# Attention, a mixture of eight experts and a cosine feed-forward layer on one core: another opening of attention, earlier reads, gates in other places, weight sums one per turn

## The chip, the cores and the metric

One core of a Trainium2 chip. The metric is the device time in microseconds (us). Before the change three runs gave 1983.06, 1985.64 and 1985.77 us, with a median of 1985.64 us.

## The reference

Three stages follow each other. All of it is float32, but the two matrices of the last stage come as float64.

```python
# attention: 4 batches, 8 heads, 576 positions, 64 wide; window of 128, a slope per head
scores = where(0 <= i - j < 128, q @ k.T / 8 - slope[h] * |i - j|, -1e9)
x = softmax(scores) @ v                     # laid out as 2304 tokens x 512
# mixture: 8 experts, 512 -> 1024 -> 512, weights by 8 rounds of row and column normalisation
P = exp(x @ w_gate - max)
for _ in range(8):
    P /= P.sum(1) + 1e-9;  P /= P.sum(0) + 1e-9;  P *= 2304 / 8
y = sum_e P[:, e] * (relu(x @ w1[e]) @ w2[e])
# feed-forward: 512 -> 2048 -> 512
h = y @ w_in;  out = (h * cos(h)) @ w_out
```

## The kernel before

Everything is written in one function under a manual schedule: each engine runs its instructions in the order in which the code issues them, and a DMA queue starts its transfers in order. Generators (`prep_a`, `prep_b`, `prep_sb`, `convert_f64`, `late_gates`, `sinkhorn` and others) hold side work. Each `yield` in them ends one step, and the main loop takes a step at fixed places, so the number of yields sets how far apart the steps stand in the program.

**Attention** (the loop from L794 on) takes 80 groups of 128 query rows of a pair of heads, two groups to a turn `i` of the loop. A turn issues the scores of its couple (`emit_qk`, TensorE matmuls into PSUM tiles `s`), the exponentials of the couple before (`emit_exp`, ScalarE), the bias and row maximum of its own (`emit_max`, VectorE, which frees the PSUM banks of the scores), `gates`, the product with v of the couple four turns back (`emit_AV`, into `xbank`), transposes of q and k of later head pairs (`heads`, which calls `emit_T`; half of them go to `xbank`, half to the pool `ps_g`), the transposes of the normalised scores three turns back (`emit_PT`, tiles `pt`), the normalisation (`emit_norm`, GpSimd) and `side`. The first scores of turns 1 and 3 use half of `xbank` and a bank of `ps_t`; all others use the two banks of `ps_s`. Heads are loaded two pairs ahead by `load_heads`, which issues two or three DMAs on SyncE's queue.

**Gates** (L367 to L384) are six products of 384 tokens with `w_gate`. `gate_block` multiplies and copies to SBUF (`lT`), `gate_block2` transposes and copies to `logits`. `gates(n)` finishes the block of the turn before and starts the next in the same turn. What attention leaves over (two blocks) is done by `late_gates` (L1248), and `sinkhorn` (L386) makes the eight rounds: a row step of four VectorE instructions (L407 to L410), a column sum on TensorE (L417), a column step of four VectorE instructions (L418 to L423).

**Mixture, first token block** (768 tokens; 32 units of 256 hidden columns). The first product uses seven sub-products instead of eight (`product`, in the order 5, 1, 4 of the unit before, 2, 3, 6, a batch, 7); every fp32 product is three matmuls of a high and a low part. A batch (`batch`, `g2`) is 36 matmuls of the second product of the unit before, for six row tiles, each followed by an accumulation on VectorE (`evac`, L1175 or L1185). Beside this the weights of later units are prepared and stored: `prep_s` sums and `prep_a` splits the first matrix into `waX` (the unit's own products read it right after the batch), `prep_b` splits the second into `wbX` (high part on ScalarE, L159, low part on GpSimd, L161), and `prep_sb` makes four sums on GpSimd (L181, "weight sums" below), their high part on ScalarE (L184), their low part on VectorE (L186), the store and the next load. The stored parts serve the later token blocks.

`convert_f64` turns float64 words into float32 with four VectorE instructions and one on ScalarE; its chunks are loaded by `load_f64` as raw 64-bit words.

Of the kernel before, what the change touches and what calls it, by code (L numbers as in the profile page):

```python
# [9 lines left out]
F32 = mybir.dt.float32  # L10
F32R = mybir.dt.float32r
I32 = mybir.dt.int32
U32 = mybir.dt.uint32
# [5 lines left out]
P = 128  # L19
# [10 lines left out]
def tile_attention_moe_cos_ffn(ctx, tc, q, k, v, w_gate, w1, w2, w_in, w_out, out):  # L30
# [41 lines left out]
    with tc.manual_schedule():  # L72
# [82 lines left out]
        def prep_b(u):  # L155
            rb = raw_t[u, "b"]
            wb = wb_of(u)
            yield
            nc.scalar.activation(out=wb[:, :, 0], in_=rb, func=AF.Copy)  # L159
            yield  # L160
            nc.gpsimd.tensor_tensor(out=wb[:, :, 1], in0=rb, in1=wb[:, :, 0].bitcast(F32), op=ALU.subtract)  # L161
            yield
            yield
            d = pair_rows(u)
            for m, f, o in ((1, 0, 0), (2, 1, 0), (4, 1, FU)):
                nc.sync.dma_start(out=d[:, SO.index(m)], in_=wb[:, f, :, o:o + FU].bitcast(F32))
            yield
# [3 lines left out]
        def prep_sb(u):  # L171
# [7 lines left out]
            for o, x, y, op in ((0, a21, a22, ALU.add), (2, raw[:, 0], a11, ALU.subtract),  # L179
                                (3, a11, a21, ALU.subtract), (1, a12, raw[:, 2], ALU.subtract)):  # L180
                nc.gpsimd.tensor_tensor(out=raw[:, o], in0=x, in1=y, op=op)  # L181
                if o in (2, 1) or not u:
                    yield
            nc.scalar.activation(out=hl[:, :, 0], in_=raw, func=AF.Copy)  # L184
            yield
# [6 lines left out]
            yield  # L192
# [61 lines left out]
        def convert_f64(c):  # L254
# [8 lines left out]
            yield  # L263
            nc.scalar.activation(out=a, in_=a, func=AF.Relu, scale=2.0 ** 23, bias=ebias)
            yield
# [4 lines left out]
            yield  # L270
            nc.vector.tensor_scalar(
                out=b, in0=hi, scalar1=0xFFFFF, scalar2=0x100000, op0=ALU.bitwise_and, op1=ALU.bitwise_or
            )
            yield
            nc.vector.scalar_tensor_tensor(
                out=w, in0=lo.bitcast(U32), scalar=2.0 ** -32, in1=b, op0=ALU.mult, op1=ALU.add
            )
# [5 lines left out]
            load_f64(c + 1)  # L283
# [238 lines left out]
        def emit_qk(n, pi, u):  # L522
            a = n % 2
            if n // 2 not in sbank:
                if n // 2 in (1, 3):
                    sbank[n // 2] = [xbank[:, :512], ps_t.tile([P, 512], F32, tag="t", name=f"s{n}_1")]
                else:
                    sbank[n // 2] = [ps_s.tile([P, 512], F32, tag="s", name=f"s{n}_{j}") for j in range(2)]
# [138 lines left out]
        load_heads(0, v, vt, "v")  # L667
# [57 lines left out]
        load_heads(1, v, vt, "v")  # L725
# [12 lines left out]
        def heads(n, pool=None):  # L738
# [3 lines left out]
            if u < 4 and pi + 1 < NP_ALL:  # L742
                emit_T(pi + 1, u, pool)
                if u == 1:
                    load_heads(pi + 2, q, qraw, "qr")
                if u == 3:
                    load_heads(pi + 2, k, kraw, "kr")

        def side(n):
# [6 lines left out]
            if n == 3:  # L756
                load_f64(0)
# [14 lines left out]
            if 8 <= n < 50 and (chunk or n < 40):  # L772
# [9 lines left out]
        def gates(n):  # L782
            nonlocal gate2, next_half
            for j, lT in gate2:
                gate_block2(j, lT, (ps_g, "g"))
            gate2 = []
            if n < NGR + 6 and next_half < 2 * NB and HB * (next_half + 1) <= done_tok:
# [6 lines left out]
        for i in range(NGR // 2 + 4):  # L794
# [9 lines left out]
            if not i:  # L804
                emit_exp(*pair(0)[0])
                emit_T(0, 1, (ps_t, "t"))
                emit_T(0, 3, (ps_g, "g"))
                emit_max(*pair(0)[1])
            for g in pair(i - 4):
                emit_AV(*g)  # L810
# [15 lines left out]
            for g in pair(i - 3):  # L826
                emit_PT(*g)
# [420 lines left out]
        def late_gates():  # L1248
            bank_ = (LastBank(), "m")
            for j in range(next_half, 2 * NB):  # L1250
                o = (1 + 2 * (j % 2)) * TB
                lT = gate_block(j, bank_, cX[:, o:o + HB])
                yield
                yield
                gate_block2(j, lT, bank_)

# [140 lines left out]
```

## Time and profile before

| what | value |
|---|---|
| three runs | 1983.06, 1985.64, 1985.77 us |
| the profiled execution, its own time | 1983.78 us |
| its span | 1982.0 us |
| PE busy / DVE / ACT / POOL | 99% / 79% / 44% / 49% |
| DMA | 540.05 MB, mean 272 GB/s |

The span runs from the first instruction to the last; 1.78 us of the profiled time lie around it. A busy PE is one whose modelled matmuls touch each other, so the 99% say how little named idle time there is, not how fast the array works. The rows in which the trace names an idle time and what ended it are what this case is read from. Attention takes the first 156 us, the first token block goes on to about 680 us.

### The profile page before, as it was taken

The numbers are of one execution on the slowest core, as the hardware profiler recorded it, in microseconds if no ns is written. First come the engines' busy times: TensorE is split into PE (matmuls) and PEld (weight loads), VectorE is DVE, ScalarE is ACT, GpSimd is POOL, SyncE is SP. The second block draws the span as 40 slices with busy tenths as digits, with TensorE's granted clock in tenths as the row PEclk, the third lists the DMA queues.
The fourth block names the chain that finished last, engine by engine and source line by source line (L and its number), as shares of the span: only waits on it lengthen the run. The fifth ranks groups of instructions, "written<-read, shape, count | busy, mean of one in ns | idle before, by whom it ended". The sixth has DMA issues, their size and how long they took to land.

```text
span 1982.0 us, 31160 instructions
## 1 busy us (share of the span) xinstructions
PE 1958.4 (99%) x10977; PEld 1823.2 (92%) x10977; DVE 1559.7 (79%) x2669; ACT 862.2 (44%) x1617; POOL 967.0 (49%) x939
## 2 busy tenths in 40 slices
PE   8999999999999999999999999999999999999999
PEld 6667899999999999999999999999999999998898
DVE  7885877777777788988988877888877776757766
ACT  6885444444444433333333433333233354554543
POOL 5673566666667545454536622545454523333221
PEclk9999999999999999999999999999999999999999
DMA  7854788888888999999999888999898765565552
GB/s 195 220 141 159 263 311 292 309 303 313 310 289 310 319 340 316 343 338 317 340 327 328 274 281 284 330 341 335 324 308 296 242 222 196 197 218 176 207 192 96
DMA packets 293755, 540.05 MB, mean 272 GB/s; under 512 B 80256, under 2 KB 141792, under 8 KB 286432
## 3 DMA queue, kind: packets, MB, share of 16 engines
q1 hardware_dynamic: 292240, 537.74, 78.6%
q8 instruction: 87, 1.43, 0.3%
q14 instruction: 68, 0.56, 0.1%
q10 hardware_dynamic: 1360, 0.33, 0.1%
HBM read 384.32 MB, written 153.67 MB: 271 GB/s over the span
## 4 chain that ended last, share of the span: by engine, by line
PE 88%; DVE 2%; DMA 1%; issue 0%; SPq 0%; POOL 0%; ACT 0%; ACTq 0%; DVEq 0%; POOLq 0%
PE gT L1105 23%; PE y_moe L966 19%; PE z_moe L966 10%; PE gT L1195 7%; PE gT L1196 7%; PE gT L1194 7%; PE y_ffn L966 5%; PE x_moe L966 5%; PE z_ffn L966 2%; PE x_ffn L966 1%; DMA wbX<-wdp 1%; SPq L96 0%; DVE waX L145 0%; DVE acc_ffn L1175 0%; DVE ta L939 0%
## 5 line engine op out<-in xcount | busy, mean ns | idle before, releaser
L1105 PE MATMUL gT<-hX,wbX 128*128 128x384 f32 x2688 | 538.3, 334 | 0.9 <-DMA wbX<-wdp 0.5
L1105 PEld LDWEIGHTS gT<-hX,wbX 128*128 128x128 f32 x2688 | 471.7, 188 | 3.5 <-DMA wbX<-wdp 1.5
L966 PE MATMUL y_moe<-xtT_moe,waX 128*128 128x384 f32 x1728 | 347.1, 335 | 0.6 <-ACT s_moe L995 0.6
L966 PEld LDWEIGHTS y_moe<-xtT_moe,waX 128*128 128x128 f32 x1728 | 304.3, 188 | 3.7 <-ACT s_moe L995 0.9
L1117 DVE TENSOR_TENSOR acc_moe<-gT,acc_moe 128x384 f32<-128x384 f32 x432 | 237.7, 550 | 77.7 <-PE gT L1105 76.0
L1196 PE MATMUL gT<-wbX,hX 128*128 128x512 f32 x660 | 258.0, 391 | 0.0
L1195 PE MATMUL gT<-wbX,hX 128*128 128x512 f32 x660 | 257.8, 391 | 0.0
L1194 PE MATMUL gT<-wbX,hX 128*128 128x512 f32 x660 | 257.7, 390 | 0.0
L995 ACT ACTIVATE s_moe<-y_moe 128x384 f32<-128x384 f32 x192 | 93.3, 486 | 345.6 <-PE y_moe L966 345.5
L1139 POOL TENSOR_TENSOR hodd<-hodd 128x384 f32<-128x384 f32 x128 | 155.4, 1233 | 139.4 <-DVE hX L1125 70.4
L1139 POOL TENSOR_TENSOR cX<-cX 128x384 f32<-128x384 f32 x128 | 146.6, 1165 | 153.6 <-DVE hX L1125 93.8
L955 POOL TENSOR_TENSOR hX<-cX,hX 128x768 fp32r<-128x768 f32 x44 | 83.5, 1914 | 249.3 <-ACT hX L952 208.6
L132 POOL TENSOR_TENSOR s<-ra 128x256 f32<-128x256 f32 x80 | 62.4, 780 | 251.3 <-DVE waX L145 178.9
L1185 DVE SCALAR_TENSOR_TENSOR acc_moe<-gT,prob,acc_moe 128x512 f32<-128x512 f32 x174 | 129.6, 747 | 37.6 <-PE gT L1196 35.8
L1196 PEld LDWEIGHTS gT<-wbX,hX 128*128 128x128 f32 x660 | 123.8, 188 | 26.0
L1194 PEld LDWEIGHTS gT<-wbX,hX 128*128 128x128 f32 x660 | 123.9, 188 | 25.4 <-DVE acc_ffn L1175 0.6
L1195 PEld LDWEIGHTS gT<-wbX,hX 128*128 128x128 f32 x660 | 123.9, 188 | 24.5
L911 ACT ACTIVATE hX<-cX 128x768 fp32r<-128x768 f32 x64 | 44.0, 687 | 218.7 <-DVE cX L998 218.7
L1125 DVE TENSOR_TENSOR hX<-cX,hX 128x768 fp32r<-128x768 f32 x112 | 132.4, 1182 | 1.1 <-ACT hX L1129 1.1
L1125 DVE TENSOR_TENSOR hX<-hodd,hX 128x768 fp32r<-128x768 f32 x112 | 127.5, 1138 | 0.9 <-ACT hX L1129 0.9
L966 PE MATMUL z_moe<-xtT_moe,waX 128*128 128x384 f32 x576 | 116.4, 335 | 0.4 <-DVE waX L145 0.2
L966 PE MATMUL z_moe<-xtB_moe,waX 128*128 128x384 f32 x576 | 115.9, 335 | 0.0
(210 smaller groups left out, 3771.9 us busy)
## 6 DMA issues: line engine op xcount, KB each, us to landing
waX<-wd SPq DMA_DIRECT2D x264, 512.0 KB, 5.5
wbX<-wdp SPq DMA_DIRECT2D x224, 512.0 KB, 6.5
wd<-waX SPq DMA_DIRECT2D x32, 1792.0 KB, 6.8
wdp<-sb SPq DMA_DIRECT2D x32, 1024.0 KB, 5.8
wdp<-wbX SPq DMA_DIRECT2D x96, 256.0 KB, 4.4
wbX<-wd SPq DMA_DIRECT2D x24, 1024.0 KB, 4.8
waX<-wd SPq DMA_DIRECT2D x88, 256.0 KB, 5.2
ra<-in_moe_w_dram SPq DMA_DIRECT2D x64, 256.0 KB, 7.4
```

Of the source, the lines that this page charges most:

```text
L132: nc.gpsimd.tensor_tensor(out=s4[:, o], in0=x, in1=y, op=op)
L955: eng.tensor_tensor(out=h[:, 1], in0=c, in1=h[:, 0].bitcast(F32), op=ALU.subtract)
L966: nc.tensor.matmul(ps[:, :HB], wa[:, WI[m], wl, kc, :], x[:, xl, kc, :], start=start and kc == 0 and n_ == 0, stop=stop and kc == 1 and n_ ...
L995: nc.scalar.activation(out=t["s", i], in_=ps[:, :HB], func=AF.Copy)
L1105: nc.tensor.matmul(ps[:, :HB], w[:, u, wl, d * P:(d + 1) * P], x[:, xl, u, :], start=m in (1, 5, 2) and n_ == 0, stop=m in (4, 3, 2) and n ...
L1117: nc.vector.tensor_tensor(out=a, in0=ps[:, :HB], in1=a, op=ALU.add)
L1125: nc.vector.tensor_tensor(out=x[:, 1], in0=H[:, q], in1=x[:, 0].bitcast(F32), op=ALU.subtract)
L1139: nc.gpsimd.tensor_tensor(out=H[:, t[0], c], in0=H[:, t[1], c], in1=H[:, t[2], c], op=ALU.subtract)
L1185: nc.vector.scalar_tensor_tensor(out=a, in0=ps, scalar=pe, in1=a, op0=ALU.mult, op1=ALU.add)
L1194: nc.tensor.matmul(ps, hf[f][:, 0, ts], wb[:, f, 0, :], start=f == 0, stop=False)
L1195: nc.tensor.matmul(ps, hf[f][:, 0, ts], wb[:, f, 1, :], start=False, stop=False)
L1196: nc.tensor.matmul(ps, hf[f][:, 1, ts], wb[:, f, 0, :], start=False, stop=f == 1)
```

## The change

- `emit_qk`: turn 1 takes both score banks from `ps_t`, turn 3 both from `ps_s`; `xbank` holds no scores any more.
- Turn 3 issues `emit_PT` ahead of the products with v and of the transposes of q and k; later turns keep it behind them.
- q and k are loaded three pairs ahead; the second pair's v is loaded in turn 2, and the first pair's v, the third pair's q and k and the first raw 64-bit words stand in turn 0.
- `convert_f64`: the second VectorE instruction moves up, the merge of the sign moves down, the next chunk is loaded two steps earlier; the first conversion starts one group later.
- `gates` finishes a block in one turn and starts the next in the following turn.
- `late_gates` has a yield ahead of each block and one behind the first.
- `prep_sb` has one sum per step and a step more ahead of its VectorE instruction, and no yield at its end.
- `prep_b`: the low part is made in two halves of 512 columns.

```diff
@@ prep_b
-            nc.gpsimd.tensor_tensor(out=wb[:, :, 1], in0=rb, in1=wb[:, :, 0].bitcast(F32), op=ALU.subtract)
+            for c in range(2):
+                nc.gpsimd.tensor_tensor(out=wb[:, c, 1], in0=rb[:, c], in1=wb[:, c, 0].bitcast(F32), op=ALU.subtract)
@@ prep_sb
                 nc.gpsimd.tensor_tensor(out=raw[:, o], in0=x, in1=y, op=op)
-                if o in (2, 1) or not u:
-                    yield
+                yield
             nc.scalar.activation(out=hl[:, :, 0], in_=raw, func=AF.Copy)
+            yield
             yield
             nc.vector.tensor_tensor(out=hl[:, :, 1], in0=raw, in1=hl[:, :, 0].bitcast(F32), op=ALU.subtract)
...
                 load_raw(u + 2, "b")
-            yield
@@ convert_f64
+            nc.vector.tensor_scalar(
+                out=b, in0=hi, scalar1=0xFFFFF, scalar2=0x100000, op0=ALU.bitwise_and, op1=ALU.bitwise_or
+            )
+            yield
             nc.scalar.activation(out=a, in_=a, func=AF.Relu, scale=2.0 ** 23, bias=ebias)
+            yield
+            nc.vector.scalar_tensor_tensor(
+                out=w, in0=lo.bitcast(U32), scalar=2.0 ** -32, in1=b, op0=ALU.mult, op1=ALU.add
+            )
             yield
             yield
             nc.vector.scalar_tensor_tensor(
                 out=a, in0=hi, scalar=-2147483648, in1=a, op0=ALU.bitwise_and, op1=ALU.bitwise_or
             )
-            yield
-            nc.vector.tensor_scalar(
-                out=b, in0=hi, scalar1=0xFFFFF, scalar2=0x100000, op0=ALU.bitwise_and, op1=ALU.bitwise_or
-            )
-            yield
-            nc.vector.scalar_tensor_tensor(
-                out=w, in0=lo.bitcast(U32), scalar=2.0 ** -32, in1=b, op0=ALU.mult, op1=ALU.add
-            )
+            load_f64(c + 1)
             yield
...
-            load_f64(c + 1)
@@ emit_qk
-                if n // 2 in (1, 3):
-                    sbank[n // 2] = [xbank[:, :512], ps_t.tile([P, 512], F32, tag="t", name=f"s{n}_1")]
-                else:
-                    sbank[n // 2] = [ps_s.tile([P, 512], F32, tag="s", name=f"s{n}_{j}") for j in range(2)]
+                pool, tag = (ps_t, "t") if n // 2 == 1 else (ps_s, "s")
+                sbank[n // 2] = [pool.tile([P, 512], F32, tag=tag, name=f"s{n}_{j}") for j in range(2)]
@@ ahead of the loop
-        load_heads(0, v, vt, "v")
...
-        load_heads(1, v, vt, "v")
@@ heads
-                    load_heads(pi + 2, q, qraw, "qr")
+                    load_heads(pi + 3, q, qraw, "qr")
...
-                    load_heads(pi + 2, k, kraw, "kr")
+                    load_heads(pi + 3, k, kraw, "kr")
@@ side
-            if n == 3:
-                load_f64(0)
+            if n == 5:
+                load_heads(1, v, vt, "v")
...
-            if 8 <= n < 50 and (chunk or n < 40):
+            if 9 <= n < 50 and (chunk or n < 40):
@@ gates
-            for j, lT in gate2:
-                gate_block2(j, lT, (ps_g, "g"))
-            gate2 = []
-            if n < NGR + 6 and next_half < 2 * NB and HB * (next_half + 1) <= done_tok:
+            if gate2:
+                for j, lT in gate2:
+                    gate_block2(j, lT, (ps_g, "g"))
+                gate2 = []
+            elif n < NGR + 6 and next_half < 2 * NB and HB * (next_half + 1) <= done_tok:
@@ the loop over turns
                 emit_T(0, 3, (ps_g, "g"))
+                load_heads(2, q, qraw, "qr")
+                load_heads(0, v, vt, "v")
+                load_heads(2, k, kraw, "kr")
+                load_f64(0)
                 emit_max(*pair(0)[1])
+            if i == 3:
+                for g in pair(i - 3):
+                    emit_PT(*g)
             for g in pair(i - 4):
                 emit_AV(*g)
...
-            for g in pair(i - 3):
-                emit_PT(*g)
+            if i > 3:
+                for g in pair(i - 3):
+                    emit_PT(*g)
@@ late_gates
                 o = (1 + 2 * (j % 2)) * TB
+                yield
                 lT = gate_block(j, bank_, cX[:, o:o + HB])
                 yield
                 yield
                 gate_block2(j, lT, bank_)
+                if j + 1 < 2 * NB:
+                    yield
```

**TensorE, turn 3 of attention.** `s` and, before, `xbank` on the left are the scores of the turn, `pt` the transposes of normalised scores, `xbank<-ident,qr` and `T<-ident,kr` the transposes of q and k of the third pair, and the last row is the first score of turn 4. Before:

```order
L537 MATMUL s_1_435<-kT_377,qT_189 128x256
L494 MATMUL xbank<-ident,qr_370 128x128 x3
L494 MATMUL T_2_463<-ident,kr_413 128x128 x2
L603 MATMUL pt_468<-ident,sp 128x128 x2
L601 MATMUL pt_468<-ident,sp 128x128
L603 MATMUL pt_471<-ident,sp 128x128
L601 MATMUL pt_468<-ident,sp 128x128
L603 MATMUL pt_471<-ident,sp 128x128
L537 MATMUL s_0_491<-kT_377,qT_189 128x256
```

And with the change:

```order
L535 MATMUL s_1_445<-kT_385,qT_189 128x256
L601 MATMUL pt_463<-ident,sp 128x128 x2
L599 MATMUL pt_463<-ident,sp 128x128
L601 MATMUL pt_466<-ident,sp 128x128
L599 MATMUL pt_463<-ident,sp 128x128
L601 MATMUL pt_466<-ident,sp 128x128
L494 MATMUL xbank<-ident,qr_329 128x128 x3
L494 MATMUL T_2_483<-ident,kr_337 128x128 x2
L535 MATMUL s_0_501<-kT_385,qT_189 128x256
```

The transposes into `xbank` move behind the six of `pt`.

**TensorE, start of the first unit of the mixture.** `gT<-xr,wg` is a late gate's product, `gT<-sel,cX` its second step; x, y and z are the unit's sub-products. Before:

```order
L966 MATMUL z_moe_0_2733<-xtT_moe_2000,waX 128x384 x6
L371 MATMUL gT_2732<-xr_87,wg 32x384 x4
L966 MATMUL y_moe_0_2749<-xtB_moe_2051,waX 128x384 x6
L380 MATMUL gT_2732<-sel,cX 128x8 x3
L371 MATMUL gT_2732<-xr_87,wg 32x384 x4
L966 MATMUL x_moe_0_2770<-xtB_moe_2110,waX 128x384 x6
L966 MATMUL z_moe_0_2733<-xtB_moe_2179,waX 128x384 x6
L380 MATMUL gT_2732<-sel,cX 128x8 x3
L966 MATMUL y_moe_0_2749<-xtT_moe_2231,waX 128x384 x6
L966 MATMUL y_moe_0_2749<-xtT_moe_2300,waX 128x384 x6
```

And with the change:

```order
L971 MATMUL z_moe_0_2737<-xtT_moe_2011,waX 128x384 x6
L971 MATMUL y_moe_0_2747<-xtB_moe_2062,waX 128x384 x6
L371 MATMUL gT_2736<-xr_87,wg 32x384 x4
L971 MATMUL x_moe_0_2763<-xtB_moe_2122,waX 128x384 x6
L380 MATMUL gT_2736<-sel,cX 128x8 x3
L971 MATMUL z_moe_0_2737<-xtB_moe_2191,waX 128x384 x6
L971 MATMUL y_moe_0_2747<-xtT_moe_2243,waX 128x384 x6
L371 MATMUL gT_2736<-xr_87,wg 32x384 x4
L971 MATMUL y_moe_0_2747<-xtT_moe_2308,waX 128x384 x6
L971 MATMUL z_moe_1_2808<-xtT_moe_2011,waX 128x384 x6
L380 MATMUL gT_2736<-sel,cX 128x8 x3
```

Each gate step has a sub-product between itself and the one before, and the second product of the gates stands between the last two sub-products.

**VectorE, the batch inside the third unit of the mixture.** `acc<-gT,acc` are the accumulations of the row tiles, L407 to L410 and L418 to L423 the two steps of the normalisation, `waX<-s` the last low part of the next unit's first matrix. Before:

```order
L410 TENSOR_TENSOR prob<-prob,gT_2732 128x144
L1175 TENSOR_TENSOR acc_moe_2889<-gT_2731,acc_moe_2889 128x512
L1175 TENSOR_TENSOR acc_moe_2889<-gT_2729,acc_moe_2889 128x512
L145 TENSOR_TENSOR waX<-ra_1933,waX 128x2x256
L1175 TENSOR_TENSOR acc_moe_2889<-gT_2730,acc_moe_2889 128x512
L145 TENSOR_TENSOR waX<-ra_1933,waX 128x256
L418 TENSOR_REDUCE gT_2732<-gT_2732 128x8
L421 TENSOR_SCALAR gT_2732<-gT_2732 128x8
L422 RECIPROCAL gT_2732<-gT_2732 128x8
L423 SCALAR_TENSOR_TENSOR prob<-prob,gT_2732 128x144
L145 TENSOR_TENSOR waX<-s_3_2932,waX 128x4x256
```

And with the change, from four rows further ahead:

```order
L410 TENSOR_TENSOR prob<-prob,gT_2736 128x144
L1180 TENSOR_TENSOR acc_moe_2888<-gT_2733,acc_moe_2888 128x512
L917 SCALAR_TENSOR_TENSOR hX<-cX,hX 128x768
L1180 TENSOR_TENSOR acc_moe_2888<-gT_2734,acc_moe_2888 128x512
L187 TENSOR_TENSOR sb<-sb 128x4x256
L1180 TENSOR_TENSOR acc_moe_2888<-gT_2735,acc_moe_2888 128x512
L1180 TENSOR_TENSOR acc_moe_2888<-gT_2733,acc_moe_2888 128x512
L418 TENSOR_REDUCE gT_2736<-gT_2736 128x8
L421 TENSOR_SCALAR gT_2736<-gT_2736 128x8
L422 RECIPROCAL gT_2736<-gT_2736 128x8
L423 SCALAR_TENSOR_TENSOR prob<-prob,gT_2736 128x144
L145 TENSOR_TENSOR waX<-ra_1944,waX 128x2x256
```

The low part of the weight sums (`sb`) comes into the batch, behind the second accumulation, in this unit and in all later ones of the block; before it stood between the batches. Behind the rows shown come an accumulation, the second `waX<-ra`, L407 to L410 and then `waX<-s`.

## Rows read from the trace of the kernel before

**Rows 1.** The page's part 1, all engines: busy us (share of the span) x instructions.
```profile
PE 1958.4 (99%) x10977; PEld 1823.2 (92%) x10977; DVE 1559.7 (79%) x2669; ACT 862.2 (44%) x1617; POOL 967.0 (49%) x939
```

**Rows 2.** Windows: engine busy us, then granted TensorE clock, DMA share, GB/s.
```profile
10.00:20.00 10.00, 6.44 (x35) 4.33 (x36) 7.28 (x37) 4.27 (x18) 3.60 (x9) 0.83 0.81 206
...
40.00:60.00 20.00, 20.00 (x172) 13.53 (x171) 16.92 (x77) 19.33 (x61) 12.33 (x24) 1.00 0.67 162
250.00:700.00 450.00, 449.96 (x2281) 409.78 (x2281) 345.28 (x464) 196.12 (x323) 282.54 (x257) 1.00 0.87 307
```

**Rows 3.** Timeline, PE, opening: start, length, work [idle before <-what ended it].
```profile
16.64 0.46 PE L537 MATMUL s<-kT,qT 64*128 64x256 f32 x1
...
18.43 0.55 PE L494 MATMUL xbank<-ident,qr 128*128 128x128 f32 x3 [1.33 <-DVE anb L547]
19.33 0.41 PE L494 MATMUL T<-ident,kr 128*128 128x128 f32 x2 [0.35 <-DMA kr<-in_k_dram]
...
20.33 0.70 PE L537 MATMUL s<-kT,qT 64*128 64x256 f32 x4
...
29.01 0.41 PE L494 MATMUL T<-ident,kr 128*128 128x128 f32 x2 [0.72 <-DMA kr<-in_k_dram]
```

**Rows 4.** Timeline, DVE, opening.
```profile
11.74 0.48 DVE L502 TENSOR_SCALAR qT<-xbank,inv 128x256 f32<-128x256 f32 x1 [0.30 <-PE xbank L494]
...
18.29 0.42 DVE L547 CUSTOM_DVE_ANT_0 sp<-s,rel 128x256 f32<-128x256 f32 x1
```

**Rows 5.** Timeline, PE, middle of attention.
```profile
64.82 0.59 PE L535 MATMUL s<-kT,qL 128*128 128x192 f32 x2 [0.53 <-DVE anb L547]
...
94.76 0.85 PE L371 MATMUL gate<-xr,wg 128*32 128x384 f32 x8 [0.72 <-DVE logits L381]
```

**Rows 6.** Timeline, PE, first unit of the mixture.
```profile
158.20 0.85 PE L371 MATMUL gT<-xr,wg 128*32 128x384 f32 x8 [0.74 <-DVE xr L655]
...
161.21 0.85 PE L371 MATMUL gT<-xr,wg 128*32 128x384 f32 x8 [0.34 <-DVE logits L381]
...
166.73 1.31 PE L966 MATMUL y_moe<-xtT_moe,waX 128*128 128x384 f32 x6 [0.58 <-ACT s_moe L995]
```

**Rows 7.** Timeline, PE, the normalisation's column sums and one product.
```profile
192.42 0.51 PE L417 MATMUL gT<-prob,ones 128*128 128x144 f32 x2 [1.21 <-DVE prob L410]
...
203.05 0.96 PE L966 MATMUL z_moe<-xtT_moe,waX 128*128 128x384 f32 x4 [0.24 <-DVE waX L145]
...
211.33 0.51 PE L417 MATMUL gT<-prob,ones 128*128 128x144 f32 x2 [1.68 <-DVE prob L410]
```

**Rows 8.** Timeline, DVE, same stretch.
```profile
188.56 1.23 DVE L186 TENSOR_TENSOR sb<-sb 128x1024 fp32r<-128x1024 f32 x1 [1.72 <-ACT sb L184]
...
191.19 0.30 DVE L407 TENSOR_REDUCE gT<-prob 128x18 f32<-128x144 f32 x1
...
192.28 0.55 DVE L998 TENSOR_TENSOR cX<-x_moe,s_moe 128x384 f32<-128x384 f32 x1
...
198.46 0.69 DVE L1175 TENSOR_TENSOR acc_moe<-gT,acc_moe 128x512 f32<-128x512 f32 x1 [0.25 <-PE gT L1196]
...
201.78 1.22 DVE L145 TENSOR_TENSOR waX<-s,waX 128x1024 fp32r<-128x1024 f32 x1
```

**Rows 9.** Timeline, a later unit of the first token block: DVE, PE, POOL.
```profile
302.56 1.67 DVE L186 TENSOR_TENSOR sb<-sb 128x1024 fp32r<-128x1024 f32 x1 [0.71 <-ACT sb L184]
...
309.79 0.75 DVE L1185 SCALAR_TENSOR_TENSOR acc_moe<-gT,prob,acc_moe 128x512 f32<-128x512 f32 x1 [0.42 <-PE gT L1196]
...
311.15 0.75 DVE L1185 SCALAR_TENSOR_TENSOR acc_moe<-gT,prob,acc_moe 128x512 f32<-128x512 f32 x1 [0.61 <-PE gT L1196]
...
313.51 1.22 DVE L145 TENSOR_TENSOR waX<-s,waX 128x1024 fp32r<-128x1024 f32 x1
...
314.74 1.20 PE L966 MATMUL z_moe<-xtT_moe,waX 128*128 128x384 f32 x6
314.81 0.74 POOL L132 TENSOR_TENSOR s<-ra 128x256 f32<-128x256 f32 x1 [5.50 <-DVE waX L145]
```

## The prediction

> **What bounds the kernel.** I read the totals first. PE is busy for 99% of the span, DVE for 79%, ACT and POOL for less than half [rows 1]. So a shorter string on another engine is worth nothing by itself: the change, which takes no matmul away, can only give back time in which PE stood still, or take more. Next come the windows [rows 2]. Between 250 and 700 us, where the first token block repeats one unit, PE is busy for 449.96 of 450 us at a granted clock of 1.00. Between 10 and 20 us it is busy for 6.44 of 10 us, at 0.83. Then the timeline, with the idle time ahead of each PE row and what ended it: that is the list of what is to be had, in the opening [rows 3], the middle of attention [rows 5], the first unit of the mixture [rows 6] and the normalisation beside the next units [rows 7]. The VectorE rows beside them [rows 4, 8, 9] say what would be late next.
>
> The sum is made against the profiled execution: 1983.78 us, of which 1982.0 are its span and 1.78 lie around it. The three runs have a median of 1985.64 us; these and the profiled one have a mean of (1983.06 + 1985.64 + 1985.77 + 1983.78) / 4 = 1984.6. One of four runs is as low as the profile, so the same program's typical time is about 0.9 us above the sum's base, and I add that at the end.
>
> **Opening of attention.** Before, turn 3's scores share `xbank` with the transposes of its own turn. The last score ends at 16.64 + 0.46 = 17.10; DVE must then finish the maxes before PE transposes into `xbank` at 18.43, after 1.33 us of idle time; k's transposes wait a further 0.35 for their DMA; the first score of turn 4 starts at 20.33 [rows 3].
> - Turn 2 comes earlier by about the 0.30 us that DVE waited for `xbank` [rows 4]: turn 1's scores no longer hold it. Turn 3's scores then end near 16.8.
> - Between 18.43 and 20.33 PE does `xbank`'s transposes, k's and `pt`: 1.90 us, less the wait for the DMA 1.55. With the change, `pt` comes first and none of it waits for turn 3's maxes, so it ends near 16.8 + 1.55 = 18.35.
> - A new wait stands behind it: turns 3 and 4 now share the two banks of `ps_s`. The last max of turn 3 ends at 18.29 + 0.42 = 18.71 before [rows 4], 18.4 with the earlier turn. So turn 4 starts near 18.45 in place of 20.33: 1.9 us.
> - The 0.72 us at 29.01, a wait for k's DMA [rows 3], goes, since k is loaded three pairs ahead.
>
> Together −2.6. From below, nothing, if these 2.6 us turn into waits for DVE or ACT; from above 2.6 plus (1 − 0.83) x 10 = 1.7 us of half clock [rows 2], if the granted clock returns sooner. I take the clock as it is, because PE still stands still in the first turns. The loads cost no PE time if they land before they are read. q, k and the first raw words are issued in turn 0, the next v's four turns before its product. q's load waits in turn 0 for PE's transposes of the first pair to free its buffer; behind it on SyncE's queue stand v, k and the raw words, none read before turn 2. If that cover is gone, the price is that of the DMA waits seen, 0.35 and 0.72 [rows 3].
>
> **Gates within attention.** A product at 94.76 waits 0.72 us, since it needs the bank that DVE's copy of the `logits` of the block before frees in the same turn [rows 5]. With one half per turn that copy is a turn old. The second half now needs ACT's copy of a turn before, not a new wait. The order differs at this one couple, later ones fall on the same matmuls. I take −0.6, between 0 and −0.72.
>
> **Conversion of float64.** The same five instructions stand in another order, so DVE's and ACT's sums don't change. The one PE wait in their neighbourhood is 0.53 at 64.82, for the maxes [rows 5]. Between 0 and −0.53 I take −0.3: maxes are DVE's string, and a lighter instruction ahead of them shortens only a part of it.
>
> **First unit.** Three waits stand there: 0.74 for `xr`'s copy, 0.34 for `logits`, 0.58 for ACT's copy of a sub-product [rows 6]. The order shows a sub-product between each gate step and the next, 1.31 us of work ahead of what had 0.34 and 0.74 to wait; the gate's product stands where ACT needs time. All three go but about 0.1: −1.6.
>
> **Normalisation.** The two waits of 1.21 and 1.68 are PE's column sums waiting for `prob` [rows 7]. Ahead of the first DVE waited 1.72 us for ACT, did `sb` for 1.23, and only then the row step, from 191.19 to 192.28, 1.09 us [rows 8]. With `sb` gone from there and the sum placed behind 24 of the batch's 36 matmuls, both go: −2.9. What is late next is the last low part, `waX<-s`. Before, it ends at 201.78 + 1.22 = 203.00 and PE waits 0.24 for it at 203.05 [rows 7, 8]. In the batches of the second and third units, DVE's string to it now has `sb` on top (1.23), less the 0.25 that DVE idles ahead of an accumulation, plus about 0.5, because a row step now stands ahead of the first accumulation: +1.5. So the wait is about 0.24 + 1.5 = 1.7, twice, 3.4 in place of 2.9 + 0.24: +0.3. From below, if DVE catches up, −3.1; from above, with the whole 1.23 and 1.09 unhidden twice, +1.5 more.
>
> **All later units.** `sb` moves into the batch in each of them. Before, it takes 1.67 us, beside POOL's sums; where POOL was still, 1.23 [rows 8, 9]. The batch has 0.42 + 0.61 = 1.03 us in which DVE waits for PE ahead of two accumulations [rows 9]. So `waX<-s`, which ends at 313.51 + 1.22 = 314.73, comes at most 1.23 − 1.03 = 0.2 late. It is read first by the third of z's six matmuls from 314.74, with the first two taking about 0.35, so 0.36 us is the margin: nothing. From below nothing too: PE has 0.04 us to give in 450 [rows 2]. From above see rival D.
>
> The trace says of the price that the same `sb` takes 1.67 beside POOL and 1.23 without [rows 8, 9], and that POOL stands idle for 5.50 us through the batch until `waX` is done [rows 9]. The Trainium skill (SBUF — State Buffer, Who interferes with whom) says that a VectorE instruction with two SBUF inputs and a GpSimd instruction that reads SBUF exclude each other, the second one blocking for the whole of the first. By that rule too the sum is unchanged as long as POOL idles there.
>
> The low part in halves adds one POOL instruction per unit; four quarter sums of 0.74 [rows 9] against one of four times the size bound it at a few tenths of a us, beside 5.50 us of idle POOL: nothing. The weight sums one per step and the extra steps move POOL's, ACT's and SyncE's work by a step or two in places where PE waits for none of them.
>
> **The sum.** −2.6 − 0.6 − 0.3 − 1.6 + 0.3 = −4.8 against 1983.78 gives 1979.0; with the 0.9 for a typical run **1980.0**, rounded up since most of these terms could be smaller.
>
> **The rivals.**
> - **B. DVE catches up in the normalisation.** Against it: DVE is nearly solid in these batches [rows 8]. For it: accumulations wait for PE there as well (0.25). Then 3.4 us more go: 1976.6. Chance 0.13.
> - **C. The opening gives nothing in the end.** ACT is busy for 19.33 of 20 us between 40 and 60 us [rows 2], so turns there may go at ACT's pace and the 1.9 us turn into waits for `sp`; against it, PE is busy for 20.00 in the same window. Or the clock stays low for a stretch as long as before (1.7 us) again. 1980.0 + 2.6 = 1982.6. Chance 0.24.
> - **D. `sb` in the batch stalls every unit.** If POOL has work there after all, now that its sums come one per step, `sb` waits for up to one whole sum: 1.23 + 0.74 = 1.97, less 1.03, is 0.94 late, less the margin of 0.36 is 0.58 a unit. Over 28 units that is +16, and 1996 us. It starts to cost from 0.36 of lateness and passes 0.2% from about 0.36 + (1985.6 + 4 − 1980) / 28 = 0.7. Against it: POOL's 5.50 us of idle time there, which the order leaves in place. By the same rule of the Trainium skill (SBUF — State Buffer) the block would be whole, not partial. Chance 0.09.
> - **E. It does less than it says.** The gates differ at one couple and the waits at 158 to 167 us return for others' copies: 1985. Chance 0.06.
>
> **How the numbers follow.** About 0.2%, 4 us, is what can be told from no change. Against 1985.64, faster means below 1981.7, slower above 1989.6. The forecast (0.48) falls below 1981.7 in 0.44, B always: 0.57 faster. C, E and 0.04 of the forecast are the same: 0.34. D: 0.09. The range leaves out D and the lower end of B, and takes in C, E and the runs' own spread: 1975.5 to 1986.5.
>
> **What would show it.** Right: the first score of turn 4 near 18.5, no idle time at k's transposes near 29 us nor at the gate near 95; the first unit without waits over 0.2; column sums without waits for `prob`, but two z products that wait about 1.7 for `waX`; PE busy for 450 of 450 between 250 and 700 us. Wrong: new waits for `sp` or DMA ahead of 60 us that return the opening's 2.6 (C); or z waiting for `waX` in every unit, with `sb` near 2 us (D).

## The result, and the profile after

Six runs of the changed kernel have a median of 2001.35 us (1997.85 to 2005.38), six of the kernel before 1985.7 us. The ratio is 1.0077, with a 95% interval of 1.0064 to 1.0089: slower by some 15 us where 6 us less were forecast. The profiled execution took 2002.06 us, its span 2000.2. PE's busy time is 5.0 us longer than in [rows 1], the span 18.2 us: most of what was added is time in which PE stands still. The page's part 1 of the changed kernel:

```profile
PE 1963.4 (98%) x10977; PEld 1824.6 (91%) x10977; DVE 1542.0 (77%) x2669; ACT 868.8 (43%) x1617; POOL 930.0 (46%) x971
```

The windows say where (PE, PEld, DVE, ACT, POOL busy us, clock, DMA share, GB/s). The first one is full, as [rows 2] was: the steady units cost nothing. The second, over the second and third token blocks, misses 11.5 us, where the kernel before misses 1.5:

```profile
240.00:600.00 360.00, 360.00 (x1815) 326.80 (x1815) 262.08 (x371) 161.09 (x258) 198.72 (x235) 1.00 0.88 307
680.00:1620.00 940.00, 928.51 (x5332) 921.69 (x5331) 786.54 (x1172) 329.64 (x563) 447.81 (x399) 1.00 0.89 311
```

The kernel before:

```profile
680.00:1620.00 940.00, 938.54 (x5409) 935.02 (x5408) 797.15 (x1190) 335.25 (x575) 446.41 (x395) 1.00 0.89 314
```

A sharper reading is to take one landmark in every unit, the start of its x product on PE's timeline, and to subtract that of the kernel before. This table does so for all profiled executions (us behind the kernel before; minus is ahead); the runs named in it are told below. "End of attention" is the start of the last product with v.

| kernel | end of attention | unit 1 | unit 7 | unit 28 | second block, first unit | third block, last unit |
|---|---|---|---|---|---|---|
| before, start in us | 155.0 | 162.0 | 255.8 | 581.5 | 659.6 | 1576.3 |
| changed | +3.5 | +0.7 | +2.3 | +2.3 | +4.9 | +18.3 |
| e1 load back | +13.1 | +10.4 | +11.9 | +11.9 | +14.5 | +15.5 |
| e2 load early, on before | +0.4 | +0.4 | +0.4 | +0.4 | +0.4 | +17.7 |
| e3 conversion old | +2.2 | -0.5 | +1.0 | +1.0 | +3.7 | +8.2 |
| e4 sums old | +5.5 | +2.7 | +6.3 | +6.3 | +6.5 | +20.7 |
| e5 conversion and loads old | -0.9 | -3.7 | -2.5 | -2.5 | +0.3 | +1.4 |
| e6 opening alone, on before | 0.0 | 0.0 | 0.0 | 0.0 | 0.0 | +3.6 |
| e7 gates alone, on before | +0.4 | -2.3 | +2.9 | +2.9 | +2.9 | +8.4 |
| e8 sums alone, on before | +0.5 | -0.3 | -0.7 | -0.7 | +2.6 | +5.9 |
| e9 load early in attention only | +2.8 | +0.1 | +1.7 | +1.6 | +4.2 | +2.6 |
| e10 and late sums old | +1.7 | -1.1 | +0.5 | +0.5 | +0.7 | +0.1 |
| e11 and raw loads later | +0.4 | -2.3 | -0.7 | -0.7 | -0.5 | +0.5 |
| e12 and conversion old | +0.3 | -2.5 | -0.9 | -0.9 | -0.7 | +2.0 |

Of the changed kernel's 18.3 us, 13.4 arise in the second and third blocks, 2.6 in the last units of the first, and 3.5 in attention. Unit 1 shows only 0.7 of these: the first unit's waits are gone, and where the late gates are the new ones, 1.4 us of their work (by the starts of the rows, 0.78 for a product and 0.58 for a second step) stands behind this landmark that stood ahead of it before. Each kernel has one profiled execution. Executions differ most in the last column, by some us, so differences of 3 us there mean little. They differ in attention by up to 4: the changed kernel, e4, e9 and e10 have the same code there and end it 1.7 to 5.5 us behind. What a kernel adds between units 1 and 28 holds to a few tenths.

**The second and third blocks.** PE's largest wait there is for the stored second matrices, `wbX<-wdp`, and it hardly existed before (0.5). With the load of raw words at its old step in these blocks it comes to 0.4 to 4.6 us in all profiled executions, with the early load (the changed kernel, e2, e4) to 10.3 to 13.1. The waits of PE, then those of SyncE's queue ahead of the loads of raw 64-bit words (L251, L245), all between 680 and 1620 us (total us, times, longest). The changed kernel:

```profile
PE gT L1110 <- DMA wbX<-wdp: 11.1, 13, 2.3
...
SPq L251 <- DVE fa L275: 64.3, 14, 6.3
SPq L245 <- DVE fa L275: 47.3, 11, 5.4
```

The kernel before:

```profile
SPq L251 <- DVE fb L275: 41.8, 14, 4.5
SPq L245 <- DVE fb L275: 25.6, 10, 3.8
```

SyncE stood for 67.4 us ahead of these loads, now for 111.6. One of them in the changed kernel, on SyncE's queue, on VectorE and on PE:

```profile
1385.57 2.56 SPq L115 DMA_DIRECT2D waX<-wd  x1
1391.48 0.33 SPq L251 DMA_DIRECT2D f<-in_moe_w_out_dram  x1
1391.91 0.44 SPq L115 DMA_DIRECT2D waX<-wd  x1
1392.39 0.47 SPq L1138 DMA_DIRECT2D wbX<-wdp  x1
...
1390.78 0.68 DVE L275 SCALAR_TENSOR_TENSOR fa<-f,fa 128x512 int32<-128x512 int32 x1
...
1396.01 1.33 PE L1110 MATMUL gT<-hX,wbX 128*128 128x384 f32 x6 [1.21 <-DMA wbX<-wdp]
...
1401.21 1.28 PE L1110 MATMUL gT<-hX,wbX 128*128 128x384 f32 x6 [0.74 <-DMA wbX<-wdp]
```

SyncE issues nothing from 1388.1 to 1391.48, until VectorE has ended its last read of the old raw words at 1391.46. Then the raw words (512 KB, needed much later) go out, and behind them `waX` and `wbX`. That `wbX` lands 8.7 us after its issue, and PE waits 0.74 us for it at 1401.21. The 1.21 us at 1396.01 is a wait for the `wbX` ahead of it, which is not in the rows: it was issued at 1382.04, as the twelfth transfer behind the stop before this one (from 1370.5 to 1375.56, ahead of two loads of raw words), and took 13.9 us to land. In the kernel before, at the same chunk, `wbX` went out ahead of the raw words:

```profile
1372.59 1.02 SPq L1133 DMA_DIRECT2D wbX<-wdp  x1
1375.50 0.33 SPq L251 DMA_DIRECT2D f<-in_moe_w_out_dram  x1
```

There it took 9.3 us to land and PE didn't wait for it, so the one that PE waited 0.74 us for was not slow but issued late. How much of the other waits is the stop itself and how much the raw words and the backlog of transfers ahead of `wbX` wasn't separated.

**Attention.** The opening gained more than forecast, lost it, and lost more. Turn 4's first score starts at 16.58 in place of 20.33 [rows 3]; the transposes that had waited 0.72 for k at 29.01 run at 24.54, 4.5 us earlier. The granted clock was 1.00 between 10 and 20 us, where [rows 2] had 0.83:

```profile
10.00:20.00 10.00, 8.38 (x62) 6.18 (x64) 9.45 (x49) 7.91 (x30) 4.96 (x13) 1.00 0.91 209
```

Then, on PE, a wait for v, and behind it a stretch at half clock (windows as above; 0.54 lies next to the lower of the two levels, 1.2 against 2.4 GHz; ahead of it PE worked 1.57 of 2 us):

```profile
16.58 0.76 PE L535 MATMUL s<-kT,qT 64*128 64x256 f32 x4
...
36.43 0.92 PE L637 MATMUL xbank<-ptT,v 128*64 128x256 f32 x4 [2.09 <-DMA v<-in_v_dram]
```

```profile
36.00:38.00 2.00, 1.57 (x8) 1.11 (x9) 0.13 (x1) 0.00 (x0) 2.00 (x4) 0.83 0.74 221
38.00:41.00 3.00, 3.00 (x17) 2.40 (x15) 0.43 (x1) 2.34 (x6) 1.20 (x3) 0.54 1.04 244
```

At 41.1 us the lead is zero: the product that stood at 41.08 before stands at 41.10. The stretch at half clock isn't needed for this: e9, with the same code there, keeps a clock of 1.00 from 36 to 53 us, and its lead is gone by 48 us (a product with v at 48.38 that stood at 47.36 before), behind a wait of 1.75 us for the maxes. VectorE had waited there for raw words and for a store, 2.50 us each.

From there to 90 us the changed kernel falls 4.5 us behind (a product with v at 90.41 before, 94.91 now). On VectorE and on PE:

```profile
79.59 0.56 DVE L260 TENSOR_SCALAR fa<-f 128x512 int32<-128x512 int32 x1 [2.99 <-DMA f<-in_moe_w_out_dram]
84.30 0.51 DVE L264 TENSOR_SCALAR fb<-f 128x512 int32<-128x512 int32 x1 [1.29 <-DMA w<-fb]
...
74.66 0.65 PE L637 MATMUL xbank<-ptT,v 128*64 128x256 f32 x4 [0.76 <-ACT wbX L159]
80.97 1.47 PE L535 MATMUL s<-kT,qT 64*128 64x256 f32 x8 [1.30 <-DVE anb L545]
85.89 0.59 PE L533 MATMUL s<-kT,qL 128*128 128x192 f32 x2 [0.95 <-DVE anb L545]
```

VectorE waits for raw words and for the store of the chunk before, and PE behind it for the maxes; in the kernel before, PE's longest wait between 70 and 90 us is 0.20.

**Normalisation.** The waits for `prob` [rows 7] are gone, and z waits for `waX` in the two units after, as forecast (1.7 each), with 0.40 and 0.32 more behind:

```profile
204.19 0.97 PE L971 MATMUL z_moe<-xtT_moe,waX 128*128 128x384 f32 x4 [1.59 <-DVE waX L145]
222.35 0.97 PE L971 MATMUL z_moe<-xtT_moe,waX 128*128 128x384 f32 x4 [1.59 <-DVE waX L145]
226.06 0.31 PE L895 MATMUL gT<-ident,prob 128*96 128x128 f32 x1 [0.40 <-DVE prob L423]
239.71 0.97 PE L971 MATMUL z_moe<-xtT_moe,waX 128*128 128x384 f32 x4 [0.32 <-DVE waX L145]
```

**Last units of the first block.** ScalarE's copy of the weight sums waits 3.20 us for POOL, which now makes the next block's token sums (`stT`) between them; an activation and VectorE's accumulations stand behind it:

```profile
603.49 1.06 ACT L184 ACTIVATE sb<-sb 128x1024 fp32r<-128x1024 f32 x1 [3.20 <-POOL sb L182]
604.45 0.47 ACT L1000 ACTIVATE s_moe<-y_moe 128x384 f32<-128x384 f32 x1
```

### The profile page after: what moved, and what is told of

Read it like the earlier page. It is cut to its first block, busy times and chain, and to the rows that moved or that the text cites. A ratio compares the mean times of both kernels' runs of the same rounds, so it can differ in the third digit from the quotient of the medians.

```text
span 2000.2 us, 31262 instructions
## 1 busy us (share of the span) xinstructions
PE 1963.4 (98%) x10977; PEld 1824.6 (91%) x10977; DVE 1542.0 (77%) x2669; ACT 868.8 (43%) x1617; POOL 930.0 (46%) x971
## 4 chain that ended last, share of the span: by engine, by line
PE 83%; DMA 7%; DVE 6%; ACT 2%; issue 2%; POOL 1%; SPq 1%; DVEq 0%; POOLq 0%; ACTq 0%
PE gT L1110 20%; PE y_moe L971 17%; PE z_moe L971 9%; PE gT L1200 6%; PE gT L1201 6%; PE gT L1199 6%; PE y_ffn L971 5%; DMA wbX<-wdp 5%; PE x_moe L971 4%; PE z_ffn L971 2%; PE xbank L637 1%; PE x_ffn L971 1%; PE s L535 1%; DMA ra<-w 1%; DVE waX L145 1%
## 5 line engine op out<-in xcount | busy, mean ns | idle before, releaser
L1110 PE MATMUL gT<-hX,wbX 128*128 128x384 f32 x2688 | 539.4, 335 | 11.5 <-DMA wbX<-wdp 11.1
L1144 POOL TENSOR_TENSOR hodd<-hodd 128x384 f32<-128x384 f32 x128 | 155.0, 1230 | 146.2 <-DVE hX L1130 77.5
L132 POOL TENSOR_TENSOR s<-ra 128x256 f32<-128x256 f32 x80 | 69.8, 873 | 199.5 <-DVE waX L145 115.8
```

The lines of the kernel that those rows point to most:

```text
L132: nc.gpsimd.tensor_tensor(out=s4[:, o], in0=x, in1=y, op=op)
L1110: nc.tensor.matmul(ps[:, :HB], w[:, u, wl, d * P:(d + 1) * P], x[:, xl, u, :], start=m in (1, 5, 2) and n_ == 0, stop=m in (4, 3, 2) and n ...
L1144: nc.gpsimd.tensor_tensor(out=H[:, t[0], c], in0=H[:, t[1], c], in1=H[:, t[2], c], op=ALU.subtract)
```

## The experiments

**Is it the place of the load?** e1 moves only the load of the changed kernel back by two steps:

```diff
-            load_f64(c + 1)
             yield
             nc.vector.scalar_tensor_tensor(out=w, ..., op0=ALU.mult, op1=ALU.mult)
             yield
+            load_f64(c + 1)
```

> The changed kernel with one line moved: the load of the next raw 64-bit words stands two steps later again, as before the change; the new order of the five conversion instructions stays. Theory L (SyncE stops at this load until VectorE has read the old words, and the weight loads of the second and third token blocks queue behind it): the 13.4 us that the changed kernel loses between 680 and 1620 us go, and PE's waits for wbX<-wdp fall from 11.1 us to under 1; about 1987 to 1989 us. Rival O (VectorE's new conversion order does it): no more than 2 us go, 1999 to 2001. Rival S (the moved weight sums and their stores leave the queue in another phase): the same, 1999 to 2001.

Measured: 1998.75 us, ratio 1.0054 (1.0039 to 1.0069). The time is neither theory's, but the table splits it: the two blocks cost 1.0 us in place of 13.4, and attention 9.7 more than in the changed kernel. VectorE waits there for raw words (7.0 us once, 5.5 once): with the first conversion one group later and the load at its old step, the load is issued a turn later (39.45 us in place of 35.32) but its words are needed in the same turn.

e2 moves only that line in the kernel before, to right behind its last reader of the raw words:

> The kernel before with that one line moved two steps earlier, right behind its last reader of the raw words, and nothing else. Theory L: slower by most of 13 us, 1995 to 1999 us, with PE waiting for wbX<-wdp some 10 us in all. Rivals O and S: no change, 1985 to 1987.

Measured: 1997.66 us, 1.0065 (1.0047 to 1.0083). The table has +17.3 us between the first unit of the second block and the last of the third, and 0.4 ahead of it; the profiled execution was one of the slower ones (2001.45), and by the medians the line costs 11 us. Its largest waits on PE, over the whole span:

```profile
PE gT L1105 <- DMA wbX<-wdp: 13.1, 10, 2.6
```

One line is enough to make the kernel before nearly as slow; rivals O and S fall.

e3 takes the whole conversion back:

> The changed kernel with the whole conversion as before: old order of the five instructions, load at its old place, first conversion one group earlier. Theory L with the conversion's own part in attention (VectorE waits 2.99 us for raw words and 1.29 for the store of the chunk before, near 80 and 84 us, and PE then 1.30 and 0.95 us for the maxes): the 13.4 us and another 2 to 3 go, 1984 to 1987. Rival O: as much as theory L, but the run with the load alone moved back shows none of it. Rival S: 1997 to 2001.

Measured: 1987.6 us, 1.0001 (0.9991 to 1.0011), 0.6 above the range. Attention is 1.2 us shorter than in the changed kernel by the table, less than the 2 to 3 that I put there and, with executions that differ by up to 4, not to be told. It still ends 2.2 us behind: VectorE waits 1.98 us for raw words there too, and PE 1.64 at 78 us for the maxes.

**The weight sums.** e4 has `prep_sb` as before in the changed kernel; e8 has the new one in the kernel before:

> The changed kernel with the weight sums as before (two sums in a step, one step less ahead of VectorE's low part). By the trace, the second and third units of the mixture wait 1.59 us each for waX and the last units of the first block, where POOL also prepares the next block's tokens, lose 2.6 us. Theory: these 2.6 go and of the normalisation up to 1 us, 13 us between 680 and 1620 us stay: 1997 to 1999. Rival S: the 13 us go too, 1984 to 1987. Rival: the waits for prob (2.9 us before) come back and eat the gain: 2000 to 2002.

> The kernel before with the new weight sums (one per step, a step more ahead of VectorE's low part) alone. Theory P (POOL's sums come later in the unit; in the last units of the first block, where POOL prepares the next tokens too, ScalarE's copy of the sums waits for them, holds up the activations behind it, and VectorE and PE follow; the stores behind are late for the second block): 2.6 us lost between 600 and 660 us and up to 2.5 more by 700, none in the units from 250 to 600 us, and nothing between 700 and 1600; against it the waits for prob become shorter by 1 to 2. In all 1988 to 1991. Rival: the second block is disturbed as in the changed kernel, 1997 or more. Rival: no difference, below 1987.5.

Measured: e4 2001.33 us, 1.0083 (1.0064 to 1.0102); e8 1989.57 us, 1.001 (1.0001 to 1.0018), in its range. The table says the same of all versions: with the new sums the units from 28 to the end of the first block lose 2.6 to 3.3 us, with the old ones 0.2 or less. In the normalisation the new sums are worth more than they cost: in e8 the column sums don't wait for `prob`, and it gains 0.4 us between units 1 and 7. e4's time is a miss for the theory and lies in the last rival's range, since with new late gates and old sums PE waits again for `prob` (0.77, 0.72), for `logits` (1.81) and for `waX` (1.14 twice), 3.6 us between units 1 and 7, which eats the 2.6.

**The gates alone** (e7: `gates` and `late_gates` of the change in the kernel before):

> The kernel before with the gates of attention and the late gates as changed, nothing else. By the prediction's steps: the waits of 0.72 at 95 us and of 0.74, 0.34 and 0.58 us in the first unit go, 2.1 us, and the waits of PE for prob come back in full, as the old weight sums stand ahead of the row step: 1984.5 against 1986.7. Rival N (the steps that the new yields move into the batches make VectorE late for waX; e4_sb_old lost 3.6 us between its first and sixth unit): no gain in all, 1986 to 1988.5.

Measured: 1987.17 us, 1.0002 (0.9994 to 1.001): rival N. The waits of [rows 5] and [rows 6] go, 2.3 us are gained at unit 1 (1.4 of them only moved), and 5.2 lost by unit 7, the moved 1.4 among them, with the same waits as in e4. Gates and sums only pay together.

**The opening.** e5 takes e3 and puts every load back to its place; e6 makes only the banks and the earlier transposes in the kernel before:

> The changed kernel with the conversion as before (as in e3_conv_old) and, besides, every load of q, k, v and of the first raw words at its place of before: q and k two pairs ahead, the second pair's v ahead of the loop. Banks, order of the transposes, gates and weight sums stay as changed. Theory Q (reading q and k a pair earlier pushes k and v back on SyncE's queue: PE waits for them at 32 and 36 us, 0.75 and 1.53 us in e3_conv_old, and the opening's gain is lost there): those waits go, PE keeps about 4 us of lead at 45 us, and the time is 2 to 4 us under e3_conv_old's 1987.6, 1984 to 1985.5. Rival A (ScalarE, near 97% busy between 40 and 60 us, takes the lead back whatever the loads do): the lead at 60 us is under 1 us again and the time as e3_conv_old, 1987 to 1988.

> The kernel before with two parts of the change alone: the score banks of turns 1 and 3, and the transposes of turn 3 ahead of the products. Loads, conversion, gates and weight sums as before. Theory Q: turn 4's first score near 16.6 us in place of 20.33, the wait of 0.72 for k at 29 us stays or grows since PE comes there earlier, and 2 to 3.7 us remain at the end: 1983 to 1984.5. Rival A: the lead is gone at 60 us, no difference from before.

Measured: e5 1987.06 us, 0.9999 (0.999 to 1.0008); e6 1986.38 us, 0.9996 (0.9988 to 1.0005): both at the time of rival A, but by waits for q and k, not by ScalarE's pace. e6 shows why: what it saves on the banks it then waits for k. On PE:

```profile
19.19 0.41 PE L494 MATMUL T<-ident,kr 128*128 128x128 f32 x2 [2.20 <-DMA kr<-in_k_dram]
19.53 0.70 PE L535 MATMUL s<-kT,qT 64*128 64x256 f32 x4
```

Turn 4 starts at 19.53, and at 29.00 PE is where it was before (29.01). Neither of my theories had this: here the opening is paced by the landing of q and k, and the new banks give time only with the earlier loads. In e5 the late waits of theory Q go, but the opening gains no more than 1.5 us at turn 4 and 0.1 at 25 us; at 65 us it has none (a score stands at 64.83, at 64.82 before [rows 5]). With conversion and loads as before, nothing is lost between 41 and 90 us either, and e5 ends attention 0.9 us ahead where e3 ended it 2.2 behind. The executions with the reads of q, k, v and the first raw words moved as in the change and the raw weight loads at their old place end it 1.7 to 13.1 behind, those with all loads as before at most 0.5: attention's loss comes with the early loads. The lead of 3.7 us at unit 1 comes from the new gates (1.4 of it only moved), and the sums take 2.9 of it back before the second block.

**Can both be had?** e9 keeps the early load for the chunks that attention converts and moves it back for the others; e10 also keeps the old weight sums from the 27th unit on:

```diff
+            if c < 4:
                 load_f64(c + 1)
...
+            if c >= 4:
+                load_f64(c + 1)
```

> The changed kernel whole, with one difference: the load of the next raw words stands early only for the first four chunks, which attention converts; from the fifth on it stands two steps later, as before the change. e1_load_back moved all of them and lost about 10 us in attention (VectorE waiting up to 7.0 us for raw words) while it lost 1.0 us in place of 13.8 between the second block's second unit and its end of the third. Theory L: attention as in the changed kernel, the second and third blocks as before: 13 us under the changed kernel, 1987 to 1989. Rival (the blocks are disturbed by the phase that attention leaves, and e1 was lucky): 1995 or more.

> As e9_load_split, and the weight sums stand as before the change from the 27th unit on; in the units ahead of it they stand as changed. Theory P (the loss between 600 and 700 us is from POOL's sums standing behind the next block's token sums): the 2.6 us up to 660 go and up to 2 more by 700: 3 to 5 us under e9_load_split, 1983 to 1985. Rival: the loss is from the sums in all units, or from the low part in halves: no difference from e9.

Measured: e9 1986.77 us, 1.0007 (0.9998 to 1.0016); e10 1984.24 us, 0.9993 (0.9984 to 1.0001). e9 is 0.2 us under its range, e10 inside its own, though 2.5 under e9 where 3 to 5 were expected. The table has no loss in the two blocks, and in e10 0.2 in place of 2.6 in the last units.

e11 then issues three of the opening's four raw weight loads (`rb` of the first unit, `ra` and `rb` of the second) at groups 24, 28 and 32; e12 is e11 with the conversion as before:

> As e10_split_sums, and three of the four raw weight loads of the opening (512 KB each) are issued at groups 24, 28 and 32 in place of 5, 6 and 7; they are first read at 72, 87 and 110 us. Theory D (k and v come late at 32 and 36 us since the DMA engines and SyncE's queue carry these loads at the same time): PE's waits for kr and v, 0.4 and 2.1 us in the changed kernel, and the stretch at half clock behind them go, and 3 to 4 of the opening's 4.4 us last: 1979 to 1982. Rival A (ScalarE's pace takes it anyway): 1983 to 1985 as e10. Rival: the moved loads delay k and v at 40 to 55 us in the same way: 1984 or more.

> As e11_raw_later, with the whole conversion as before the change (old order of the instructions, load at its old place, first conversion one group earlier). In e11_raw_later PE holds 3.0 us of lead at 55 us and has none left at 79 us, after 1.35 and 1.33 us of waits for the maxes; on VectorE the conversion stands ahead of these maxes and waits 0.93 and 1.44 us for the store of the chunk before and 3.01 for raw words. Theory V (the moved second instruction overwrites the buffer that the store still reads, and the raw words come late): these two waits go and 2 to 3 us stay with the kernel, 1980 to 1981.5. Rival A (ScalarE's pace takes the lead): 1982.5 to 1983.5 as e11_raw_later.

Measured: e11 1982.95 us, **0.9985 (0.9976 to 0.9993)**, the only version whose interval lies clear of 1 on the better side; e12 1984.73 us, 0.9991 (0.9982 to 1.0). In e11 the wait for v and the half clock behind it are gone, and the lead is 4.4 us at 34 us and 3.0 at 52. So theory D holds for the wait, not for the price: 1982.95 lies between its range and rival A's lower end, and by 83 us the lead is gone. e12, which should have kept it, lies above both its ranges: it goes from 4.05 us ahead at 72 to 0.2 behind at 79 and 1.3 behind at 84. There VectorE waits for raw words, PE for the maxes, and the clock halves:

```profile
72.00:78.00 6.00, 3.11 (x20) 2.19 (x22) 2.32 (x11) 2.08 (x7) 3.94 (x6) 0.86 1.05 283
78.00:84.00 6.00, 6.00 (x38) 4.88 (x34) 4.71 (x20) 4.50 (x17) 3.30 (x7) 0.57 0.63 142
```

```profile
75.68 0.55 DVE L264 TENSOR_SCALAR fa<-f 128x512 int32<-128x512 int32 x1 [4.21 <-DMA f<-in_moe_w_out_dram]
...
77.07 2.42 PE L539 MATMUL s<-kT,qT 64*128 64x256 f32 x8 [2.89 <-DVE anb L549]
```

The raw words took 9.0 us to land: e12 issues them at 66.69 and reads them at 75.68; the kernel before issues them at 66.86 and reads them at 75.66, when it comes to them without a wait. Theory V's waits for the store did go; the one for raw words grew from 3.01 to 4.21 us. The kernel before has the same burst of transfers, with DMA shares of 0.98 and 0.99 at the same place:

```profile
66.00:72.00 6.00, 6.00 (x55) 4.30 (x55) 5.61 (x26) 3.97 (x15) 4.07 (x8) 1.00 0.98 325
72.00:78.00 6.00, 5.67 (x46) 3.59 (x42) 4.55 (x24) 6.00 (x19) 3.41 (x8) 1.00 0.99 277
```

In e12, the lead that PE brings to this place meets transfers that come no sooner, and the half clock behind the wait takes some more. Whether the store of `waX` (1792 KB) that stands in the burst could move wasn't tried.

## Why the prediction was wrong

- **The conversion is the step that failed.** I wrote that "the same five instructions stand in another order, so DVE's and ACT's sums don't change", and priced it by the one PE wait near it in attention. I counted the moved load only as a load that lands in time, and only in the opening. It is issued again in the second and third blocks, some 25 times, ahead of the weight loads on SyncE's queue and with a wait for VectorE in front of it. That is 13.4 us in the profile; e2 makes 17.3 in its profile (11 by the medians) with one line, and e1 and e9 take it away. In attention too the new conversion waits for its words and its store (2.99 and 1.29 us).
- **Opening, −2.6:** the wait for the bank and its place were right, and the size was 4.5 us by 29 us (3.75 at turn 4). Nearly all of it hangs on the early loads (e6 has 0.8 at turn 4 and nothing at 29 us), and the clock, which I left at 0.83, was 1.00. The term that failed is the price of these loads, put at nothing, or at 0.35 and 0.72 us if their cover was gone. "None read before turn 2" was no answer for v: the earlier reads of q and k and the raw weight loads push v back, and PE waits 2.09 us for it. Without the raw weight loads there the wait and the half clock are gone (e11). By 41 us the lead is zero, by 90 us the kernel is 4.5 behind; e3 and e5, which differ in the loads, end attention 2.2 behind and 0.9 ahead. Rival C had the outcome as far as 41 us, but by ScalarE's pace or the clock alone; late transfers, of v above all, were not in it.
- **Gates, −0.6, and first unit, −1.6:** right. The waits of 0.72, 0.74, 0.34 and 0.58 are gone. The gates gave 0.8 us between 90 and 108 us, the first unit 2.3 by its first batch (from 3.50 behind to 1.22).
- **Normalisation, +0.3:** right in kind and near in size. z waits 1.59 twice where I had 1.7; the 0.40 and 0.32 behind were missing: +1.1 between the first batch (1.22 us behind) and the fifth (2.28). The upper bound should have said 1.6 more, not 1.5: (1.23 + 1.09 − 1.5) x 2.
- **Later units, 0:** right from 243 to 602 us, where the lag stays at 2.28 to the hundredth; rival D, with its block of `sb`, did not occur. Wrong for the last units, where POOL has the next block's token sums to make: 2.6 us that "PE waits for none of them" passed over.
- Together: attention +3.5 where −3.5 were forecast, first unit −2.3, normalisation +1.1, last units +2.6, the two blocks +13.4, in all the 18.3 of the table.
- The slower side came, with nearly the price of rival D, but by another mechanism; that the price was near is chance.

## What to carry to other kernels

In this kernel a DMA issue that had to wait for VectorE held up the transfers behind it on SyncE's queue, so moving one earlier in the program is priced by what stands behind it, at every place where it repeats and not only at the one where the change is wanted. Time won ahead of a stretch that transfers pace was lent here and not given: before counting it, look at the next loads and at the DMA share of the windows behind. Side work that pays in the middle of a loop can cost at its end, where other side work joins it; a version that switches there (e10) is cheap to try.

## What the runs showed of the hardware

A pause of 2.09 us on PE at 36 us was followed by a stretch at a granted clock of 0.54, and in e12 one of 2.89 us at 77 us by one at 0.57, so that the wait cost more than its own length: 2.9 us of waiting became a loss of 4.2 by 79 us and 5.4 by 84. The length of the last pause alone doesn't tell whether the clock falls: behind 1.64 us at 78 us in e3 it was 0.56, behind 1.75 us at 47 us in e9 it stayed at 1.00.

In e12, 512 KB took 9.0 us to land in a stretch with a DMA share near 1, so that a PE four us ahead met them at the same time as one that was not.

SyncE, held at one load until VectorE had read the old words, issued nothing from 1388.1 to 1391.48, and a transfer behind it landed 8.7 us after its issue and too late for PE by 0.74 us.
